# Another prologue for a two-layer attention and MLP kernel: input ahead of weights, a fixed order for the first norm, V by two token tiles, scratch matmuls, and other places for the next inputs

## The chip, the cores and the metric

The kernel runs on one core of one Trainium2 chip. The metric is device time in microseconds (us), as the median of several executions. "PE" is the matmul engine, "PEld" its weight load, "DVE" the vector engine, "ACT" the scalar engine, "POOL" the third compute engine, and "SP" the engine from which most DMAs are issued.

## The reference, cut to what matters

```python
def reference(A_x, A_wqkv, A_wo, B_x, B_W_gate, B_W_up, B_W_down):
    # A: 32 heads of 32; every token attends to 8 earlier tokens, 2 apart
    # B: relu(x @ W_gate) * (x @ W_up) @ W_down
    x = A_x                                    # 1 x 2048 x 1024, bf16
    x = x + _A_ref(_layernorm(x), A_wqkv, A_wo)
    x = x + _B_ref(_layernorm(x), B_W_gate, B_W_up, B_W_down)
    x = x + _A_ref(_layernorm(x), A_wqkv, A_wo)
    x = x + _B_ref(_layernorm(x), B_W_gate, B_W_up, B_W_down)
    return x
```

## The kernel before

The 2048 tokens are worked on in four blocks of 512 (four tiles of 128). The host code of the kernel builds a list of pairs (time, function) called `ev`, sorts it by time and calls the functions in that order; the times are the author's plan, in us. Instructions of PE and the DMAs of SP are chained in the order of these calls. Other engines' instructions are put in order by the framework's scheduler unless `tc.issue_after` fixes it.

In all the argument, a *group* is eight matmuls of 512 columns, one for each eighth of the 1024 inputs. At full rate a group takes 1.73 us.

The prologue is what comes before the first Q matmul: load block 0, normalise its four tiles (statistics of two on DVE, of two on ACT), turn them with PE transposes (eight a tile), copy the turned tiles out, and compute V of block 0 in eight groups.

```python
    def load_x(b):
        for t in range(b * TPB, (b + 1) * TPB):
            if b == 0 and t % 2:
                nc.scalar.dma_start(x_tiles[t][:], x_dram[t * P:(t + 1) * P, :])
            else:
                sp_dma(x_tiles[t][:], x_dram[t * P:(t + 1) * P, :])

    load_x(0)
    # ... (cut)
    def ln_first():
        hold = {"xnT": xnT_pool.tile([P, TPB, KC, P], BF16, tag="xnT", name="xnT_first")}
        xna = big_tile([P, TPB, D], "xn_first", True)
        for t in range(TPB):
            xt = x_tiles[t]
            xn = xna[:, t, :]
            if t % 2 == 0:
                mv, rstd = ln_dve_stats(xt)
                nc.vector.tensor_scalar(xn, xt[:], mv[:, 0:1], rstd[:], op0=ALU.subtract, op1=ALU.mult)
            else:
                # ... (cut: sums by two ACT passes, small operations on DVE, power on POOL)
                nc.scalar.activation(xn, xt[:], ACT.Identity, scale=rstd[:], bias=nb[:])
            tp = psum.tile([P, KC, P], BF16, tag="acc", name="tp")
            for c in range(KC):
                nc.tensor.transpose(tp[:, c, :], xn[:, c * P:(c + 1) * P], ident[:])
            if t % 2 == 0:
                nc.vector.tensor_copy(hold["xnT"][:, t, :, :], tp[:])
            else:
                nc.scalar.copy(hold["xnT"][:, t, :, :], tp[:])
        return hold
    # ... (cut)
    def v_steps(n, ln, key, early=False):
        # ... one of these for each of the 8 column chunks c:
                for kc in range(KC):
                    mm(acc[:], lhsT=slab[(key, g)][:, kc, col:col + P], rhs=ln["xnT"][:, :, kc, :],
                       start=(kc == 0), stop=(kc == KC - 1))
                tail_act[0] = nc.scalar.copy(st["vT"][:, c, :], acc[:]).ins
    # ... (cut: the plan of block 0)
    t_v0 = 17.0
    ev.append((0.45, lambda: load_x(1)))
    spread(v_steps(0, ln_a[0], "v0", early=True), t_v0, GRP)
    ln1(1, 18.0, t_qk0 + 2.0, True, 2.6, range(TPB))
    ev.append((t_qk0 - 4.0, lambda: load_x(2)))
    # ... products of q and k on DVE (mults), their reductions L on PE (reds)
    ev.append((t_qk1 + 0.5 * GRP, reds[KC - 2]))
    ev.append((t_qk1 + 1.5 * GRP, reds[KC - 1]))
    ev.append((t_qk1 + 1.6 * GRP, lambda: softmax(0)))
    ln1(2, 37.0, t_qk1 + 2.0, True, 4.5)
```

## Time and profile before

| | before |
|---|---|
| median of 3 executions | 1636.67 us (1636.62 to 1637.32) |
| span in the profile | 1635.0 us |
| PE busy | 1616.4 us |
| first transpose, first V matmul, first Q matmul | 8.81, 15.04, 30.95 us |
| V of block 0, from its first matmul to the first Q | 15.91 us, where 8 x 1.73 = 13.84 is due |

PE is busy 99% of the span, so time can be won only where PE idles or runs slowly. The list of PE's waits in the kernel before says where it idles (columns: what waited, for what, us in total, times, longest):

```profile
PE tp L298 <- DVE xn_first L280: 8.8, 1, 8.8
PE tp L298 <- ACT xn_first L295: 1.2, 2, 0.9
PE acc_v L120 <- ACT xnT_first L302: 1.1, 1, 1.1
PE dacc L120 <- DVE x L582: 0.8, 1, 0.8
PE L L120 <- DVE prod L395: 0.5, 1, 0.5
```

Three of the five belong to the prologue. The last is a reduction L that waits for the last product of block 0. The timeline of PE in the kernel before shows them in place (start, us from first to last, engine, line, operation, out<-in, sizes, count, and in brackets the idle time before it and what ended it):

```profile
8.81 1.03 PE L298 MATMUL tp<-ident,xn_first 128*128 128x128 bf16 x8 [8.81 <-DVE xn_first L280]
...
15.04 16.07 PE L120 MATMUL acc_v<-xnT_first,w_v 128*128 128x512 bf16 x64 [1.10 <-ACT xnT_first L302]
30.95 1.89 PE L120 MATMUL acc_q<-xnT_first,w_qk_q 128*128 128x512 bf16 x8
...
62.78 1.89 PE L120 MATMUL acc_q<-xnT_a,w_qk_q 128*128 128x512 bf16 x8
64.60 0.62 PE L120 MATMUL L<-prod,sel 128*32 128x512 bf16 x8
65.15 1.95 PE L120 MATMUL acc_q<-xnT_a,w_qk_q 128*128 128x512 bf16 x8
67.63 0.62 PE L120 MATMUL L<-prod,sel 128*32 128x512 bf16 x8 [0.54 <-DVE prod L395]
...
147.66 1.89 PE L120 MATMUL acc_g<-xnT_b,w_g 128*128 128x512 bf16 x8
```

What this line does not show is that V starts slowly. The weight loads of V in the kernel before, from the timeline of PEld, do: a weight load accompanies each matmul, so the distance between two of them is the time of a matmul.

```profile
15.42 0.15 PEld L120 LDWEIGHTS <-w_v 128*128 128x128 bf16 x1 [0.28 <-issue]
15.85 0.15 PEld L120 LDWEIGHTS <-w_v 128*128 128x128 bf16 x1 [0.28 <-issue]
```

They lie 0.427 us apart up to 19.3 us, and 0.216 us apart from then on: half rate, then full rate. The page's row of granted clock is full in this stretch all the same, so it cannot be taken as the proof that PE runs at full rate early in a kernel.

### The profile page before, as it was taken

The numbers are of one execution on the slowest core, as the hardware profiler recorded it, in microseconds if no ns is written. First come the engines' busy times: TensorE is split into PE (matmuls) and PEld (weight loads), VectorE is DVE, ScalarE is ACT, GpSimd is POOL, SyncE is SP. The second block draws the span as 40 slices with busy tenths as digits, with TensorE's granted clock in tenths as the row PEclk, the third lists the DMA queues.
The fourth block names the chain that finished last, engine by engine and source line by source line (L and its number), as shares of the span: only waits on it lengthen the run. The fifth ranks groups of instructions, "written<-read, shape, count | busy, mean of one in ns | idle before, by whom it ended". The sixth has DMA issues, their size and how long they took to land.

```text
span 1635.0 us, 18583 instructions
## 1 busy us (share of the span) xinstructions
PE 1616.4 (99%) x7527; PEld 777.6 (48%) x7576; DVE 1060.9 (65%) x923; ACT 507.7 (31%) x1047; POOL 255.7 (16%) x220
## 2 busy tenths in 40 slices
PE   7999999999999999999999999999999999999999
PEld 3554445444554445444454444544445444444444
DVE  3699999986397936949279492794828948211211
ACT  5745322433241423405134051340513311131110
POOL 2411103301160102201052010520105100000000
PEclk9999999999999999999999999999999999999999
DMA  9569557755567475764856647577474764655451
GB/s 297 93 179 240 163 170 217 197 161 175 178 187 203 155 209 167 197 177 155 232 162 185 178 151 230 179 185 215 150 226 160 205 204 154 206 156 179 155 166 66
DMA packets 371222, 296.81 MB, mean 182 GB/s; under 512 B 142400, under 2 KB 351296, under 8 KB 370240
## 3 DMA queue, kind: packets, MB, share of 16 engines
q1 hardware_dynamic: 370848, 295.10, 62.0%
q8 instruction: 59, 0.97, 0.3%
q10 hardware_dynamic: 288, 0.52, 0.1%
q14 instruction: 27, 0.22, 0.0%
HBM read 256.77 MB, written 21.00 MB: 170 GB/s over the span
## 4 chain that ended last, share of the span: by engine, by line
PE 92%; DVE 4%; ACT 2%; issue 1%; DMA 1%; POOL 0%; ACTq 0%; SPq 0%; DVEq 0%
PE acc_g L120 24%; PE acc_u L120 24%; PE dacc L120 22%; PE acc_v L120 6%; PE acc_wo L120 6%; PE acc_k L120 5%; PE acc_q L120 5%; DVE t L423 2%; DVE ac L433 1%; DMA x<-in_A_x_dram 1%; ACT xn_a L227 1%; ACT xn_a L228 1%; DVE pv L485 0%; PE L L120 0%; DVE x L530 0%
## 5 line engine op out<-in xcount | busy, mean ns | idle before, releaser
L120 PE MATMUL acc_g<-xnT_b,w_g 128*128 128x512 bf16 x1792 | 423.4, 379 | 0.0
L120 PE MATMUL acc_u<-xnT_b,w_u 128*128 128x512 bf16 x1792 | 423.3, 379 | 0.0
L120 PE MATMUL dacc<-w_d,hT 128*128 128x512 bf16 x1759 | 386.5, 379 | 2.5 <-DVE x L582 0.8
L554 ACT ACTIVATE r<-acc_g 128x512 bf16<-128x512 f32 x224 | 133.5, 596 | 746.9 <-PE acc_g L120 746.7
L555 DVE TENSOR_TENSOR hT<-acc_u,r 128x512 bf16<-128x512 f32 x224 | 153.7, 686 | 314.2 <-PE acc_u L120 313.4
L120 PEld LDWEIGHTS <-hT 128*128 128x128 bf16 x1792 | 175.3, 98 | 212.4 <-issue 1.1
L120 PEld LDWEIGHTS <-w_g 128*128 128x128 bf16 x1792 | 174.8, 98 | 212.8 <-issue 3.0
L120 PEld LDWEIGHTS <-w_u 128*128 128x128 bf16 x1792 | 175.4, 98 | 211.4
L423 DVE TENSOR_TENSOR t<-q,k 128x2048 f32<-128x2048 bf16 x84 | 191.7, 2290 | 8.6 <-ACT k L362 5.8
L433 DVE TENSOR_TENSOR ac<-ac,t 128x2048 f32<-128x2048 f32 x84 | 191.8, 2283 | 0.4
L367 POOL COPY kh<-k 128x14 bf16<-128x14 bf16 x64 | 82.1, 1288 | 480.5 <-ACT k L362 480.5
L582 DVE TENSOR_TENSOR x<-dacc,x 128x512 bf16<-128x512 f32 x64 | 42.5, 687 | 164.0 <-PE dacc L120 164.0
L485 DVE TENSOR_TENSOR pv<-a,vhm 128x4096 bf16<-128x4096 bf16 x64 | 145.2, 2282 | 0.0
L120 PE MATMUL acc_wo<-w_o,oT 128*128 128x512 bf16 x496 | 111.0, 379 | 0.8
L232 POOL TENSOR_TENSOR st_b<-st_b,neg_half 128x1 f32<-128x1 f32 x29 | 56.5, 1957 | 297.9 <-ACT st_b L231 297.9
L232 POOL TENSOR_TENSOR st_a<-st_a,neg_half 128x1 f32<-128x1 f32 x32 | 40.5, 1273 | 318.1 <-ACT st_a L231 317.9
L366 POOL COPY k<-kh 128x14 bf16<-128x14 bf16 x48 | 71.3, 1485 | 65.4 <-DVE t L423 43.8
L120 PEld LDWEIGHTS <-oT 128*128 128x128 bf16 x512 | 50.1, 98 | 60.3
L486 DVE TENSOR_TENSOR pv<-pv 128x2048 bf16<-128x2048 bf16 x64 | 77.4, 1214 | 0.2
L358 ACT CAST q<-acc_q 128x512 bf16<-128x512 f32 x64 | 37.6, 587 | 72.9 <-PE acc_q L120 72.9
L322 ACT CAST vT<-acc_v 128x512 bf16<-128x512 f32 x64 | 37.4, 585 | 70.8 <-PE acc_v L120 70.8
L227 ACT ACTIVATE xn_b<-x 128x1024 bf16<-128x1024 bf16 x29 | 30.3, 1046 | 92.1 <-DVE x L530 92.1
(125 smaller groups left out, 1204.5 us busy)
## 6 DMA issues: line engine op xcount, KB each, us to landing
w_g<-in_B_W_gate_dram SPq DMA_DIRECT2D x56, 1024.0 KB, 6.6
w_u<-in_B_W_up_dram SPq DMA_DIRECT2D x56, 1024.0 KB, 5.3
w_d<-in_B_W_down_dram SPq DMA_DIRECT2D x48, 1024.0 KB, 5.7
w_o<-in_A_wo_dram SPq DMA_DIRECT2D x16, 1024.0 KB, 7.1
vhm<-v_d SPq DMA_DIRECT2D x32, 284.0 KB, 6.8
v_d<-vT SPq DMA_DIRECT2D x8, 1024.0 KB, 9.6
oT<-o_d SPq DMA_DIRECT2D x32, 256.0 KB, 4.3
w_d<-in_B_W_down_dram SPq DMA_DIRECT2D x16, 512.0 KB, 4.2
```

Of the source, the lines that this page charges most:

```text
L120: tail_pe[0] = nc.tensor.matmul(*args, **kwargs).ins
L227: nc.scalar.activation(xn, xt[:], ACT.Square, accum_out=sq)
L232: nc.gpsimd.tensor_tensor(rstd, vpe, neg_half[:, 0:1], op=ALU.pow)
L366: nc.gpsimd.tensor_copy(k[:, 0:HALO], khalo[n - 1][:, c, :])
L367: nc.gpsimd.tensor_copy(khalo[n][:, c, :], k[:, BLK:BLK + HALO])
L423: nc.vector.tensor_tensor(t[:], i0, i1, op=ALU.mult)
L433: nc.vector.tensor_tensor(o, ac[:], t[:], op=ALU.add)
L485: nc.vector.tensor_tensor(tt[:], a_bc, v_sh, op=ALU.mult)
L486: nc.vector.tensor_tensor(tt[:, 0:4], tt[:, 0:4], tt[:, 4:8], op=ALU.add)
L554: tail_act[0] = nc.scalar.activation(r[:], acc[:], ACT.Relu).ins
L555: nc.vector.tensor_tensor(hold["hT"][:, j, :], accs["u"][:], r[:], op=ALU.mult)
L582: nc.vector.tensor_tensor(xs, ac[t], xs, op=ALU.add)
```

## The change

Its intent is to have V, and so the long unbroken stream of PE, begin sooner and at full rate. It has seven parts:

- (a) Tile 0 of the input comes in two halves, one on each of two queues; tile 2 comes on the ACT queue, tiles 1 and 3 on SP's (before: 1 and 3 on ACT's, 0 and 2 on SP's).
- (b) The norm of block 0 runs in a fixed order on each engine (`on`, `dv`); tiles 0, 1 and 3 have their statistics on DVE, tile 2 on ACT.
- (c) Fourteen scratch matmuls of ones run on PE while it has nothing to do. Nothing reads their result.
- (d) V is computed for tiles 0 and 1 first (chunks 0 to 5), then for tiles 2 and 3, then chunks 6 and 7 for all four. Tiles 2 and 3 are turned inside V.
- (e) The inputs of blocks 1 and 2 are both asked for after the fourth slab of Q and K weights: for block 2 that is sooner, for block 1 later. The norm of block 1 is interleaved with block 0's products in a fixed order.
- (f) The last L reduction and the softmax of block 0 come one group later.
- (g) Loads for the PV stage, the ACT statistics of blocks 2 and 3 and the input of block 3 move later. One small ACT instruction on the ones is new too (not shown); the ACT table load that it could bring forward starts at 1.70 us in both kernels.

```diff
@@ loading (a)
-            if b == 0 and t % 2:
+            if t == 0:
+                sp_dma(x_tiles[t][:, 0:SLAB], x_dram[t * P:(t + 1) * P, 0:SLAB])
+                nc.scalar.dma_start(x_tiles[t][:, SLAB:D], x_dram[t * P:(t + 1) * P, SLAB:D])
+            elif t == 2:
                 nc.scalar.dma_start(x_tiles[t][:], x_dram[t * P:(t + 1) * P, :])
@@ scratch (c) and order (b)
+    ones = const.tile([P, SLAB], BF16, name="ones")
+    nc.vector.memset(ones[:], 1.0)
+    def scratch(count):
+        sc = psum_l.tile([P, W, P], F32, tag="L", name="scratch")
+        for _ in range(count):
+            with pe_group():
+                mm(sc[:, 0:WH, :], lhsT=ones[:, 0:P], rhs=ones[:], start=True, stop=True)
@@ ln_first (helpers cut; "v" is DVE, "a" is ACT)
+        scratch(14)
+        bn(0, 0)
+        bn(0, 1)
+        aggr(0)
+        bn(1, 0)
+        bn(1, 1)
+        aggr(1)
+        st1 = act_stats(2)
+        apply(0)
+        turn(0)
+        apply(1)
+        copy(0, "v", 0, KC // 2)
+        copy(0, "a", KC // 2, KC)
+        turn(1)
+        act_vpe(2, st1)
+        copy(1, "v", 0, KC // 2)
+        copy(1, "a", KC // 2, KC)
+        bn(3, 0)
+        bn(3, 1)
+        apply(2)
+        aggr(3)
+        apply(3)
+        hold["later"] = {2: (lambda: (turn(2), copy(2, "a"))),
+                         4: (lambda: (turn(3), copy(3, "v", 0, KC // 2), copy(3, "a", KC // 2, KC)))}
@@ v_first (d)
+        plan = [(c, 0, 2) for c in range(6)] + [(c, 2, 4) for c in range(6)] + [(c, 0, 4) for c in range(6, KC)]
+        # for each (c, t0, t1): cols = slice(t0 * P, t1 * P)
+                        mm(acc[:, cols], lhsT=slab[("v0", c // 4)][:, kc, (c % 4) * P:(c % 4 + 1) * P],
+                           rhs=ln["xnT"][:, t0:t1, kc, :], start=(kc == 0), stop=(kc == KC - 1))
@@ the plan (e), (f), (g)
-    t_v0 = 17.0
+    t_v0 = 9.5
-    ev.append((0.45, lambda: load_x(1)))
-    ln1(1, 18.0, t_qk0 + 2.0, True, 2.6, range(TPB))
-    ev.append((t_qk0 - 4.0, lambda: load_x(2)))
+    ev.append((t_v0 + GRP * 5 + 0.5, lambda: load_x(1)))
+    ev.append((t_v0 + GRP * 5 + 0.6, lambda: load_x(2)))
+    # ... statistics, apply and turn of block 1, one tile at a time
-    ev.append((t_qk1 + 1.5 * GRP, reds[KC - 1]))
-    ev.append((t_qk1 + 1.6 * GRP, lambda: softmax(0)))
-    ln1(2, 37.0, t_qk1 + 2.0, True, 4.5)
+    ev.append((t_qk1 + 2.5 * GRP, reds[KC - 1]))
+    ev.append((t_qk1 + 2.6 * GRP, lambda: softmax(0)))
+    ln1(2, t_qk0 + 10.0, t_qk1 + 5.0, True, 4.5)
```

More of the change, by code (lines that the diff above doesn't have):

```diff
@@ L1 @@
-from contextlib import ExitStack, contextmanager
+from contextlib import ExitStack, contextmanager, nullcontext
 import concourse.bass as bass
@@ L95, with dv @@
     tail_pe = [None]
+    tail_dve = [None]
+    def dv(f, *args, **kwargs):
+        if tail_dve[0] is None:
+            tail_dve[0] = f(*args, **kwargs).ins
+        else:
+            with tc.issue_after(tail_dve[0]):
+                tail_dve[0] = f(*args, **kwargs).ins
     tail_sp = [None]
@@ L223, in f @@
                 if t in dve:
-                    hold[t] = ln_dve_stats(xt)
+                    hold[t] = ln_dve_stats(xt, which == "a")
                     return
                 sx, sq, nm2, vpe, rstd, mr = (hold["st"][:, t, i:i + 1] for i in range(6))
-                nc.scalar.activation(xn, xt[:], ACT.Square, accum_out=sq)
-                nc.scalar.activation(xn, xt[:], ACT.Identity, accum_out=sx)
+                with (tc.issue_after(tail_act[0]) if early else nullcontext()):
+                    nc.scalar.activation(xn, xt[:], ACT.Square, accum_out=sq)
+                    nc.scalar.activation(xn, xt[:], ACT.Identity, accum_out=sx)
                 nc.scalar.activation(nm2, sx, ACT.Square, scale=1.0 / D)
@@ L239, in f @@
                     mv, rstd = hold[t]
+                    if which == "a":
+                        dv(nc.vector.tensor_scalar, hold["xn"][:, t, :], x_tiles[b * TPB + t][:], mv[:, 0:1], rstd[:],
+                           op0=ALU.subtract, op1=ALU.mult)
+                        return
                     gate[0] = nc.vector.tensor_scalar(hold["xn"][:, t, :], x_tiles[b * TPB + t][:], mv[:, 0:1], rstd[:],
@@ L258, in ln_steps, with ln_dve_stats, run @@
         return [stats(t) for t in range(TPB)], [apply(t) for t in range(TPB)], turn, hold
-    def ln_dve_stats(xt):
+    def ln_dve_stats(xt, ordered):
+        def run(f, *args, **kwargs):
+            if ordered:
+                dv(f, *args, **kwargs)
+            else:
+                f(*args, **kwargs)
         bst = stat_pool.tile([P, 2, 6], F32, tag="bst", name="bst")
-        nc.vector.bn_stats(bst[:, 0, :], xt[:, 0:512])
-        nc.vector.bn_stats(bst[:, 1, :], xt[:, 512:1024])
+        run(nc.vector.bn_stats, bst[:, 0, :], xt[:, 0:512])
+        run(nc.vector.bn_stats, bst[:, 1, :], xt[:, 512:1024])
         mv = stat_pool.tile([P, 2], F32, tag="mv", name="mv", bufs=4)
-        nc.vector.bn_aggr(mv[:], bst[:].rearrange("p a b -> p (a b)"))
+        run(nc.vector.bn_aggr, mv[:], bst[:].rearrange("p a b -> p (a b)"))
         vpe = stat_pool.tile([P, 1], F32, tag="vpe1", name="vpe1")
-        nc.vector.tensor_scalar(vpe[:], mv[:, 1:2], EPS, None, op0=ALU.add)
+        run(nc.vector.tensor_scalar, vpe[:], mv[:, 1:2], EPS, None, op0=ALU.add)
         rstd = stat_pool.tile([P, 1], F32, tag="rstd1", name="rstd1", bufs=4)
@@ L274, in ln_first @@
         xna = big_tile([P, TPB, D], "xn_first", True)
-        for t in range(TPB):
-            xt = x_tiles[t]
-            xn = xna[:, t, :]
-            if t % 2 == 0:
-                mv, rstd = ln_dve_stats(xt)
-                nc.vector.tensor_scalar(xn, xt[:], mv[:, 0:1], rstd[:], op0=ALU.subtract, op1=ALU.mult)
-            else:
-                st1 = stat_pool.tile([P, 2], F32, tag="st1", name="st1")
-                nc.scalar.activation(xn, xt[:], ACT.Identity, accum_out=st1[:, 0:1])
-                nc.scalar.activation(xn, xt[:], ACT.Square, accum_out=st1[:, 1:2])
-                mean = stat_pool.tile([P, 1], F32, tag="mean1", name="mean1")
-                nc.vector.tensor_scalar(mean[:], st1[:, 0:1], 1.0 / D, None, op0=ALU.mult)
-                nvar = stat_pool.tile([P, 1], F32, tag="nvar1", name="nvar1")
-                nc.vector.scalar_tensor_tensor(nvar[:], st1[:, 0:1], mean[:], st1[:, 1:2], op0=ALU.mult, op1=ALU.subtract)
-                vpe = stat_pool.tile([P, 1], F32, tag="vpe1", name="vpe1")
-                nc.vector.tensor_scalar(vpe[:], nvar[:], -1.0 / D, EPS, op0=ALU.mult, op1=ALU.add)
-                rstd = stat_pool.tile([P, 1], F32, tag="rstd1", name="rstd1", bufs=4)
-                nc.gpsimd.tensor_tensor(rstd[:], vpe[:], neg_half[:, 0:1], op=ALU.pow)
-                nb = stat_pool.tile([P, 1], F32, tag="nb1", name="nb1")
-                nc.vector.scalar_tensor_tensor(nb[:], mean[:], -1.0, rstd[:], op0=ALU.mult, op1=ALU.mult)
-                nc.scalar.activation(xn, xt[:], ACT.Identity, scale=rstd[:], bias=nb[:])
-            tp = psum.tile([P, KC, P], BF16, tag="acc", name="tp")
-            for c in range(KC):
-                nc.tensor.transpose(tp[:, c, :], xn[:, c * P:(c + 1) * P], ident[:])
-            if t % 2 == 0:
-                nc.vector.tensor_copy(hold["xnT"][:, t, :, :], tp[:])
-            else:
-                nc.scalar.copy(hold["xnT"][:, t, :, :], tp[:])
@@ new lines, in ln_first, with on, small @@
+        last = {}
+        def on(eng, f, *args, **kwargs):
+            if eng == "v":
+                dv(f, *args, **kwargs)
+            elif eng in last:
+                with tc.issue_after(last[eng]):
+                    last[eng] = f(*args, **kwargs).ins
+            else:
+                last[eng] = f(*args, **kwargs).ins
+        def small(name, bufs=4):
+            return stat_pool.tile([P, 1], F32, tag="f" + name, name=name, bufs=bufs)
+        mean, vpe, rstd, bst = {}, {}, {}, {}
@@ new lines, in bn, with aggr @@
+        def bn(t, half):
+            if half == 0:
+                bst[t] = stat_pool.tile([P, 2, 6], F32, tag="bst", name="bst")
+            on("v", nc.vector.bn_stats, bst[t][:, half, :], x_tiles[t][:, half * SLAB:(half + 1) * SLAB])
+        def aggr(t):
+            mv = stat_pool.tile([P, 2], F32, tag="mv", name="mv", bufs=4)
+            on("v", nc.vector.bn_aggr, mv[:], bst[t][:].rearrange("p a b -> p (a b)"))
+            vpe[t], mean[t] = small("vpe1"), mv[:, 0:1]
+            on("v", nc.vector.tensor_scalar, vpe[t][:], mv[:, 1:2], EPS, None, op0=ALU.add)
+            power(t)
@@ new lines, in power, with act_stats, act_vpe @@
+        def power(t):
+            rstd[t] = small("rstd1")
+            on("g", nc.gpsimd.tensor_tensor, rstd[t][:], vpe[t][:], neg_half[:, 0:1], op=ALU.pow)
+        def act_stats(t):
+            st1 = stat_pool.tile([P, 2], F32, tag="st1", name="st1")
+            on("a", nc.scalar.activation, xna[:, t, :], x_tiles[t][:], ACT.Identity, accum_out=st1[:, 0:1])
+            on("a", nc.scalar.activation, xna[:, t, :], x_tiles[t][:], ACT.Square, accum_out=st1[:, 1:2])
+            return st1
+        def act_vpe(t, st1):
+            mn = small("mean1")
+            on("v", nc.vector.tensor_scalar, mn[:], st1[:, 0:1], 1.0 / D, None, op0=ALU.mult)
+            nvar = small("nvar1")
+            on("v", nc.vector.scalar_tensor_tensor, nvar[:], st1[:, 0:1], mn[:], st1[:, 1:2], op0=ALU.mult, op1=ALU.subtract)
+            vpe[t], mean[t] = small("vpe1"), mn[:]
+            on("v", nc.vector.tensor_scalar, vpe[t][:], nvar[:], -1.0 / D, EPS, op0=ALU.mult, op1=ALU.add)
+            power(t)
@@ new lines, in apply, with turn, copy @@
+        def apply(t):
+            on("v", nc.vector.tensor_scalar, xna[:, t, :], x_tiles[t][:], mean[t], rstd[t][:],
+               op0=ALU.subtract, op1=ALU.mult)
+        tps = {}
+        def turn(t):
+            tps[t] = psum.tile([P, KC, P], BF16, tag="acc", name="tp")
+            for c in range(KC):
+                with pe_group():
+                    tail_pe[0] = nc.tensor.transpose(tps[t][:, c, :], xna[:, t, c * P:(c + 1) * P], ident[:]).ins
+        def copy(t, eng, c0=0, c1=KC):
+            f = nc.vector.tensor_copy if eng == "v" else nc.scalar.copy
+            on(eng, f, hold["xnT"][:, t, c0:c1, :], tps[t][:, c0:c1, :])
@@ new lines, in ln_first @@
+        warm = small("warm")
+        on("a", nc.scalar.activation, warm[:], ones[:, 0:1], ACT.Identity)
+        scratch(14)
[16 more added lines that the diff above has]
+        bn(3, 0)
@@ L325, in v_steps, with v_first, f_, f @@
         return [f_(c) for c in range(KC)]
+    def v_first(ln):
+        st = att[0]
+        plan = [(c, 0, 2) for c in range(6)] + [(c, 2, 4) for c in range(6)] + [(c, 0, 4) for c in range(6, KC)]
+        def f_(i, c, t0, t1):
+            def f():
+                if i == 0:
+                    st["vT"] = big_tile([P, KC, BLK], "vT_0", True)
+                acc = psum.tile([P, BLK], F32, tag="acc", name="acc_v")
+                cols = slice(t0 * P, t1 * P)
+                with pe_group():
+                    for kc in range(KC):
+                        mm(acc[:, cols], lhsT=slab[("v0", c // 4)][:, kc, (c % 4) * P:(c % 4 + 1) * P],
+                           rhs=ln["xnT"][:, t0:t1, kc, :], start=(kc == 0), stop=(kc == KC - 1))
+                tail_act[0] = nc.scalar.copy(st["vT"][:, c, cols], acc[:, cols]).ins
+                if i in ln["later"]:
+                    ln["later"][i]()
+            return f
+        at, out = 0.0, []
+        for i, (c, t0, t1) in enumerate(plan):
+            out.append((at, f_(i, c, t0, t1)))
+            at += GRP * (t1 - t0) / TPB
+        return out
     def store_v(n):
@@ L394, in f @@
                 i0, i1 = qk_bcast(n, c, 0, W)
-                nc.vector.tensor_tensor(prods[c][:], i0, i1, op=ALU.mult)
+                dv(nc.vector.tensor_tensor, prods[c][:], i0, i1, op=ALU.mult)
             return f
@@ L598 @@
     GRP = 1.73
-    GRP = 1.73
     def spread(steps, at, gap):
@@ L642 @@
     t_gu0 = t_v3 + GRP * KC
-    want_v("v0", t_v0 + GRP * KC / 2, t_qk0)
+    want_v("v0", t_v0 + GRP * 5, t_qk0)
     want_qk("qk01", t_v1)
     want_v("v123", t_v3 + GRP * KC / 2, t_gu0)
-    ev.append((0.45, lambda: load_x(1)))
-    ev.append((0.5, zero_v))
-    spread(v_steps(0, ln_a[0], "v0", early=True), t_v0, GRP)
-    ln1(1, 18.0, t_qk0 + 2.0, True, 2.6, range(TPB))
-    ev.append((t_qk0 - 4.0, lambda: load_x(2)))
+    for at, f in v_first(ln_a[0]):
+        ev.append((t_v0 + at, f))
+    ev.append((t_v0 + GRP * 5 + 0.5, lambda: load_x(1)))
+    ev.append((t_v0 + GRP * 5 + 0.6, lambda: load_x(2)))
+    ev.append((t_v0 + GRP * 5 + 0.7, zero_v))
+    stats, apply, turn, ln_a[1] = ln_steps(1, "a", True, range(TPB))
+    for t in range(TPB):
+        ev.append((t_qk0 + (1.0, 2.0, 2.2 * GAP0, 4.2 * GAP0)[t], stats[t]))
+        ev.append((t_qk0 + (1.9 + 2 * t) * GAP0 - 0.1, apply[t]))
+        ev.append((t_qk0 + (1.9 + 2 * t) * GAP0, turn(t)))
     ev.append((t_qk0 + 1.5, store_v(0)))
-    ev.append((t_qk0 + 2.1, lambda: load_x(3)))
+    ev.append((t_qk0 + 18.0, lambda: load_x(3)))
     spread(qk_steps(0, ln_a[0], "qk01"), t_qk0, GAP0)
@@ L659 @@
             ev.append((t_qk0 + GAP0 * (2 * c + 4.5), reds[c]))
-    spread(load_v_steps(0), t_qk0 + 5.0, 6.0)
+    spread(load_v_steps(0), t_qk0 + 19.0, 1.0)
     ev.append((t_qk1 + 0.5 * GRP, reds[KC - 2]))
-    ev.append((t_qk1 + 1.5 * GRP, reds[KC - 1]))
-    ev.append((t_qk1 + 1.6 * GRP, lambda: softmax(0)))
-    ln1(2, 37.0, t_qk1 + 2.0, True, 4.5)
+    ev.append((t_qk1 + 2.5 * GRP, reds[KC - 1]))
+    ev.append((t_qk1 + 2.6 * GRP, lambda: softmax(0)))
+    ln1(2, t_qk0 + 10.0, t_qk1 + 5.0, True, 4.5)
     spread(qk_steps(1, ln_a[1], "qk01"), t_qk1, GRP)
```

## The prediction

> **What bounds the kernel now.** The page's first part has PE busy 1616 of 1635 us. The list of waits charges PE with five: 8.8 us for the first normalised tile, 1.2 for the next, 1.1 for the transposed input, 0.54 at one L reduction (67 us), 0.8 at a down projection (314 us). The timeline has the first V matmul at 15.04 us and the first Q matmul at 30.95; from there PE hardly stops, 1.73 us per eight 512-column matmuls. So the change can win only what lies before 31 us, plus small waits.
>
> V takes 15.9 us where 8 x 1.73 = 13.8 is due: until about 19 us its weight loads lie 0.427 us apart, later 0.216. The matmuls run at half rate though the granted clock reads 1.0, as the Trainium skill says ("TensorE: Matmul & The Clock Gate", "The HAM clock gate": cold until about 3.4 us of sustained activity). That costs 2.1 us.
>
> **What changes, costed.**
> 1. Before, four tiles are normalised and turned before any V: x lands at 4.5-5.7, first transpose 8.81, last copy ends 15.0. Now V needs tiles 0 and 1 only. From about 4.0: two statistics (0.62 each) and two small operations, to 5.7; tile 1's during tile 0's 0.55-0.8 us power, to 7.3; apply 0.55, to 8.0; transposes 0.6-0.9; small operations and half copies; V at 10.2 (estimate). W_v's first slab should land near 8.5: by then 2.1 MB had moved before.
> 2. Fourteen scratch matmuls (14 x 0.427 = 6 us) on an idle PE: V starts warm, the 2.1 us goes.
> 3. V pays: 16 transposes now sit inside it (1-1.7 us), 48 more matmuls cost little each. V: 13.8 + 1.7 = 15.5, ending near 25.7 against 30.95: 5.2 us won. Tiles 2 and 3 should be applied near 13.4, needed near 15.
> 4. Block 1's input now queues behind a slab that waits for W_v: it lands around 26-28. Its statistics and applies (8 us of DVE) move among block 0's eight products (2.3 us each, one per 4.1 us of PE): 26 of 33 us. Room enough. ACT was full from 36 to 60 us with statistics of blocks 2 and 3; block 3's now come later, so K copies and products are punctual.
> 5. The last L reduction comes one group later: the 0.54 us wait goes, but softmax starts 1.1 us later relative to PE. DVE is full from 75 to 200 us, so its chain gains 4 us while PE gains 5.7. The attention output's first tile landed near 117.4, PE takes it at 120.0: 2.6 us of slack, 1.6 used. DVE idles 6 us before 207 and catches up.
>
> **Sum.** 5.2 + 0.54 = about 5.8 us: 1636.7 - 5.8 = **1630.9 us**. Eight in ten: 1629.2 to 1633.0. Chances: faster by over 2% 0.005, within 2% 0.99, slower 0.005.
>
> **What would show it.** First V matmul at 9.4-11 us (1); 256-column matmuls about 0.11 us apart from the start (2); first Q near 25.7 (3); no PE wait on products or block 1's input, block 1's Q starting near 57 instead of 62.8 (4, 5); no PE wait before the output projection near 114; from 250 us everything shifted by the same 5-6 us, the 0.8 us wait kept.
>
> **What would make it wrong.** x or W_v landing later; PE cold again between scratch and transposes (up to 2 us); 256-column matmuls bound by weight loads (+1 us or more); block 1's late input pushing products and softmax until the output projection waits; the MLP input's DMA transposes, with under 2 us of slack at 147.7, coming late.

## The result, and the profile after

Four executions of each kernel were taken in the same rounds. Ratios in this document are the mean time of one kernel's fast runs over that of the other's of the same rounds, so not quite the ratio of the medians.

| | before | after |
|---|---|---|
| median (lowest to highest) | 1636.97 us (1636.62 to 1637.32) | 1630.12 us (1630.08 to 1630.63) |
| ratio | | 0.9959 (95%: 0.9944 to 0.9973) |
| span in the profile | 1635.0 | 1628.4 |
| first transpose | 8.81 | 7.45 |
| first V matmul | 15.04 | 9.69 |
| first Q matmul | 30.95 | 24.69 |
| first Q of block 1 | 62.78 | 56.52 |
| first gate matmul of block 0 | 147.66 | 140.79 |

The kernel is 0.4% faster: 6.85 us between the medians, where 5.8 were predicted. That is within the 2% that count as the same here, but the interval of the ratio leaves out 1. The list of PE's waits in the changed kernel:

```profile
PE scratch L129 <- DVE ones L296: 1.5, 1, 1.5
PE dacc L129 <- DVE x L700: 0.8, 1, 0.8
PE acc_v L129 <- DVE xnT_first L103: 0.6, 1, 0.6
PE tp L364 <- DVE xn_first L103: 0.4, 1, 0.4
```

What was 8.8 + 1.2 + 1.1 is now 1.5 + 0.6 + 0.4. The first of these is a wait before scratch work, so it costs nothing by itself, and the scratch matmuls have turned idle time into busy time of no use: busy PE has to be read by tile here. The L wait is gone, and the 0.8 of the down projection stays. The timeline of PE in the changed kernel (columns as above):

```profile
1.52 5.91 PE L129 MATMUL scratch<-ones 128*128 128x512 bf16 x14 [1.52 <-DVE ones L296]
7.45 0.62 PE L364 MATMUL tp<-ident,xn_first 128*128 128x128 bf16 x8
8.44 0.62 PE L364 MATMUL tp<-ident,xn_first 128*128 128x128 bf16 x8 [0.37 <-DVE xn_first L103]
9.69 2.96 PE L129 MATMUL acc_v<-xnT_first,w_v 128*128 128x256 bf16 x24 [0.63 <-DVE xnT_first L103]
12.48 0.61 PE L364 MATMUL tp<-ident,xn_first 128*128 128x128 bf16 x8
12.93 1.91 PE L129 MATMUL acc_v<-xnT_first,w_v 128*128 128x256 bf16 x16
14.68 0.61 PE L364 MATMUL tp<-ident,xn_first 128*128 128x128 bf16 x8
15.12 9.73 PE L129 MATMUL acc_v<-xnT_first,w_v 128*128 128x256 bf16 x72
24.69 1.89 PE L129 MATMUL acc_q<-xnT_first,w_qk_q 128*128 128x512 bf16 x8
...
56.52 1.89 PE L129 MATMUL acc_q<-xnT_a,w_qk_q 128*128 128x512 bf16 x8
58.34 0.62 PE L129 MATMUL L<-prod,sel 128*32 128x512 bf16 x8
58.88 3.67 PE L129 MATMUL acc_q<-xnT_a,w_qk_q 128*128 128x512 bf16 x16
62.49 0.62 PE L129 MATMUL L<-prod,sel 128*32 128x512 bf16 x8
...
140.79 1.89 PE L129 MATMUL acc_g<-xnT_b,w_g 128*128 128x512 bf16 x8
```

Three things are to be seen. V starts 15.04 - 9.69 = 5.35 us sooner. From V's first matmul to the first Q it takes 24.69 - 9.69 = 15.0 us instead of 15.91; eight transposes now take 0.62 us instead of 1.03, so PE is at full rate when they come. And the second L reduction (62.49) has no bracket, hence no wait. From here the sum closes: 5.35 + 0.91 + 0.54 = 6.80, and the gate matmuls come 147.66 - 140.79 = 6.87 us sooner. Nothing of it is given back later: the 0.8 us wait of the down projection moved from 315.03 to 308.13 us, by 6.90.

One input of this is the first statistics on DVE. First the line of the kernel before, from the timeline of DVE:

```profile
4.71 0.69 DVE L262 BATCH_NORM_STATS2 bst<-x 128x6 f32<-128x512 bf16 x1 [4.71 <-DMA x<-in_A_x_dram]
```

and that of the changed kernel, from the same view:

```profile
3.60 0.69 DVE L100 BATCH_NORM_STATS2 bst<-x 128x6 f32<-128x512 bf16 x1 [2.13 <-DMA x<-in_A_x_dram]
```

The half tile gets there 1.1 us sooner than the whole one did.

### The profile page after: what moved, and what is told of

It is laid out like the page before. It is cut to its first block, busy times and chain, and to the rows that moved or that the text cites. A ratio compares the mean times of both kernels' runs of the same rounds, so it can differ in the third digit from the quotient of the medians.

```text
span 1628.4 us, 18703 instructions
## 1 busy us (share of the span) xinstructions
PE 1618.6 (99%) x7589; PEld 782.2 (48%) x7638; DVE 1062.6 (65%) x926; ACT 506.1 (31%) x1050; POOL 255.7 (16%) x220
## 4 chain that ended last, share of the span: by engine, by line
PE 95%; DVE 4%; issue 1%; DMA 0%; POOL 0%; DVEq 0%
PE acc_g L129 24%; PE acc_u L129 24%; PE dacc L129 22%; PE acc_v L129 7%; PE acc_k L129 6%; PE acc_q L129 6%; PE acc_wo L129 6%; DVE t L541 2%; DVE ac L551 1%; PE L L129 1%; DVE pv L603 0%; DVE x L648 0%; DVE pv L604 0%; DVE ac L541 0%; DMA x<-in_A_x_dram 0%
## 5 line engine op out<-in xcount | busy, mean ns | idle before, releaser
L480 ACT CAST k<-acc_k 128x512 bf16<-128x512 f32 x64 | 37.3, 583 | 63.0 <-PE acc_k L129 62.8
```

## The experiments

The profile says what moved. It does not say which of the parts moved it, because several of them act on the same few microseconds. Twelve kernels were run. The table has all of them. "Against before" is the median less the median of the kernel before on the same chip; those medians lay between 1636.70 and 1637.24 us, so differences below half a microsecond between rows of different chips are not read. The starts of V and Q are from the profiled execution, one for each kernel. The interval of the ratio includes 1, no change, for e2, e3 and e9.

| run | median us | against before | first V | first Q |
|---|---|---|---|---|
| changed kernel | 1630.12 | -6.85 | 9.69 | 24.69 |
| e1_no_scratch | 1631.76 | -5.48 | 10.10 | 26.37 |
| e2_before_scratch | 1638.38 | +1.14 | 15.77 | 31.98 |
| e3_no_split | 1635.81 | -1.43 | 14.46 | 30.22 |
| e4_red_early | 1630.14 | -7.10 | 9.66 | 24.67 |
| e5_x0_whole | 1632.44 | -4.57 | 10.67 | 27.00 |
| e6_free_order | 1632.48 | -4.53 | 11.06 | 26.74 |
| e7_x1_early | 1630.84 | -6.17 | 9.89 | 24.89 |
| e8_scratch_20 | 1630.58 | -6.43 | 9.61 | 24.62 |
| v1_single_tile | 1632.21 | -4.49 | 9.71 | 26.52 |
| e9_before_fill | 1635.72 | -1.17 | 15.30 | 29.11 |
| e10_no_split_fill | 1633.56 | -3.33 | 14.36 | 28.17 |
| v2_hold_back | 1631.46 | -5.43 | 9.71 | 26.16 |

All gave correct results. At first the theory was that of the prediction: the parts act one by one and add up (an earlier V, plus about 2 us for a PE that is at full rate when V starts). The rivals were that one part does nearly all, or that parts hang together.

### e1: the changed kernel without scratch matmuls

```diff
-        scratch(14)
```

> The changed kernel without its 14 scratch matmuls. Theory A (the scratch matmuls warm PE's clock): the 32 transposes and the first V groups run at half rate for about 4 us of PE activity, as in the kernel before: the first V matmul moves from 9.69 to about 10.2 us, weight loads of V's first groups lie about 0.213 us apart instead of 0.11, Q starts near 27.2 instead of 24.69; time 1632.2 to 1633.0 (2.1 to 2.8 us more than the changed kernel). Rival B (the transposes warm PE anyway, or the half rate of before had another cause): V at 9.7 to 10.2 with 0.11 us spacing from the start, time within 0.7 us of 1630.1.

Measured: 1631.76 us (1631.39 to 1632.37), less than expected. The first V matmuls in this kernel, from the timeline of PE, are to be compared with 2.96 us for the same 24 in the changed kernel:

```profile
10.10 4.22 PE L129 MATMUL acc_v<-xnT_first,w_v 128*128 128x256 bf16 x24 [0.52 <-DVE xnT_first L103]
```

The scratch matmuls are worth 1.68 us of Q's start: 4.22 - 2.96 = 1.26 for V's first matmuls, and 0.41 for V's start (the first transpose is 0.11 later, and from there to V takes 0.30 longer). The prediction had read 2.1 us for a cold V from the kernel before; here a cold V costs 1.26, so that price is not a constant.

### e2: the kernel before with scratch matmuls and nothing else

```diff
     def ln_first():
         # ...
+        scratch(17)
         for t in range(TPB):
```

> The kernel before with 17 scratch matmuls ahead of its first transposes and nothing else of the change. Theory A: first V matmul still near 15 us (14.6 to 15.0, as transposes run at full rate), but V takes 13.8 instead of 15.9 us: Q starts near 28.6 instead of 30.95; time 1634.3 to 1635.0. Rival B: V still 15.9 us, time 1636.5 to 1637.3. If the wait at the last L reduction grows because ACT stays where it was, up to 0.5 us of the gain is lost there (then 1635.0 to 1635.5).

Measured: 1638.38 us (1637.51 to 1638.77), ratio 1.0006 (0.9991 to 1.0021). The expectation fell: not faster at all. The windows of this kernel show what happened (columns: stretch, its length, busy us and count of PE, PEld, DVE, ACT, POOL, then granted clock, DMA share and GB/s). The stretches are 3.41 us long and laid so that one ends where the clock fell, at 13.83 us by the clock record of the trace (it keeps the moments at which the granted clock changed):

```profile
7.00:10.41 3.41, 1.67 (x13) 0.74 (x11) 2.06 (x12) 2.85 (x6) 1.96 (x4) 1.00 1.10 355
10.41:13.83 3.42, 1.19 (x18) 1.02 (x19) 1.85 (x5) 1.91 (x3) 0.55 (x1) 1.00 1.07 375
13.83:17.24 3.41, 2.31 (x12) 1.24 (x11) 0.00 (x0) 1.73 (x2) 0.00 (x0) 0.50 1.05 387
17.24:20.65 3.41, 3.41 (x9) 1.22 (x8) 0.00 (x0) 0.59 (x1) 0.00 (x0) 0.50 1.05 388
```

The granted clock is 0.50 from 13.83 to 20.65 us. PE was brought to full rate by the scratch matmuls, then had little to do (transposes that wait for the norm), and fell back to half rate 1.9 us before V began at 15.77. So V took 31.98 - 15.77 = 16.2 us, as slow as before, and it also began 0.73 us later (why was not traced). From this came a third theory: *scratch matmuls are worth something only if PE is kept busy from them to the real stream; the early start of V is what keeps it busy.* It is tested by e9 and e10.

### e3: the changed kernel with V whole

```diff
-        hold["later"] = {2: (lambda: (turn(2), copy(2, "a"))),
-                         4: (lambda: (turn(3), copy(3, "v", 0, KC // 2), copy(3, "a", KC // 2, KC)))}
+        turn(2)
+        copy(2, "a")
+        turn(3)
+        # ... copies of tile 3
+        hold["later"] = {}
-        plan = [(c, 0, 2) for c in range(6)] + [(c, 2, 4) for c in range(6)] + [(c, 0, 4) for c in range(6, KC)]
+        plan = [(c, 0, 4) for c in range(KC)]
```

> The changed kernel with V in eight groups of 512 columns after all four tiles, all else kept. Theory A: V begins when tile 3 is copied, near 13.9 us instead of 9.69, and takes 13.8 us instead of 15.16: Q near 27.7 instead of 24.69, time 1632.8 to 1633.4 (about 3 us more). Rival (the split is not worth its transposes and half matmuls, the fixed order and the loads are what counts): time within 1 us of 1630.1.

Measured: 1635.81 us (1635.6 to 1636.0). Without the split only 1.4 us of the gain are left, far less than expected. The clock fell here too, for 6.8 us from 11.6 on, so V took 15.76 us.

### e9: the kernel before, with scratch matmuls also between the transposes

```diff
+        scratch(17)
         for t in range(TPB):
             # ... after the transposes of tile t
+            scratch((5, 0, 7, 5)[t])
```

> The run of the kernel before with scratch matmuls came out slower, not faster: its granted clock fell to 0.50 from about 13.9 to 20.4 us, after the transposes had left PE idle for most of 8 to 14 us. Theory C: once warmed, PE is set back to half rate when it idles too much over some us, so scratch matmuls ahead of the norm only pay if PE then stays busy. Here 5, 7 and 5 scratch matmuls more fill the gaps after the transposes, nothing else changes. C: granted clock 1.0 throughout, V's weight loads 0.216 us apart from its first group, V takes 13.8 us instead of 16.2; V starts at 15.8 to 16.2 us and Q at 29.6 to 30.1; time 1635.4 to 1636.4, 2 to 3 us under the run without the fill. Rival D (the clock falls at about 14 us whatever PE does, say by the all-ones data or a fixed time after warming): clock 0.50 again and time 1638 to 1639.

Measured: 1635.72 us (1635.36 to 1635.95), 1.2 us under the kernel before (ratio 0.9991, 0.9978 to 1.0005) and, each against the kernel before on its chip, 2.3 us under e2. All four executions have a mean clock of 1.000, where e2's four have 0.996 to 0.999. The windows of this kernel (columns as above):

```profile
8.31:11.72 3.41, 2.68 (x30) 1.84 (x31) 1.99 (x7) 1.82 (x3) 1.75 (x4) 1.00 1.10 354
11.72:15.13 3.41, 3.23 (x22) 1.47 (x20) 0.76 (x2) 2.93 (x3) 0.19 (x1) 1.00 1.05 386
```

The clock stays up, and V takes 29.11 - 15.30 = 13.8 us, the 8 x 1.73 that are due. The third theory holds: what e2 lacked was work for PE between the scratch matmuls and V. Q starts 1.84 us sooner than before, of which 1.2 us arrive at the end; PE waits 0.9 us for L reductions instead of 0.54, and the rest was not traced.

### e10: e3 with scratch matmuls filling the same gaps

```diff
         turn(1)
+        scratch(9)
         # ...
         turn(2)
+        scratch(3)
         # ...
         turn(3)
+        scratch(4)
```

> The changed kernel with V whole after four tiles came out 5.7 us slower, where I expected 3: its clock too fell to 0.50, from about 11.8 to 18.2 us. Here 9, 3 and 4 scratch matmuls fill PE's gaps between the transposes. Theory C: clock 1.0 throughout, V starts near 14.0 to 14.5 us (the first two pairs of transposes and copies at full rate), takes 13.8 us, Q near 28.0 to 28.4; time 1633.2 to 1633.8, 2 to 2.5 us under the run without the fill; the split of V itself is then worth 3.1 to 3.7 us and the clock that it keeps up the rest. Rival D: clock 0.50 again, time about 1635.8.

Measured: 1633.56 us (1633.32 to 1633.88). The same stretch in both kernels, first in e3:

```profile
8.19:11.60 3.41, 0.92 (x14) 0.75 (x15) 3.17 (x11) 1.17 (x2) 0.55 (x1) 1.00 1.10 364
```

and in e10:

```profile
8.19:11.60 3.41, 2.71 (x21) 1.33 (x20) 3.24 (x10) 1.17 (x2) 0.55 (x1) 1.00 1.09 365
```

With 0.92 us busy the clock fell at 11.6; with 2.71 it stayed at 1.00. e10 gives the split its own price. With the clock up in both, the first Q is at 28.17 us without the split and at 24.69 with it: 3.5 us for starting V on two tiles instead of four. The remaining 2.05 us of e3's loss (30.22 - 28.17) are the clock's.

### e5: the changed kernel, tile 0 in one piece

```diff
-            if t == 0:
-                sp_dma(x_tiles[t][:, 0:SLAB], x_dram[t * P:(t + 1) * P, 0:SLAB])
-                nc.scalar.dma_start(x_tiles[t][:, SLAB:D], x_dram[t * P:(t + 1) * P, SLAB:D])
-            elif t == 2:
+            if b == 0 and t % 2:
```

> The changed kernel with block 0's input loaded as before: tile 0 whole on one queue, tiles 1 and 3 on the other, tile 2 on the first. Theory: tile 0 in two halves at the heads of both queues is what brought the first statistics from 4.71 to 3.60 us, and the chain of tile 1 carries this to V. So here the first statistics start at 4.5 to 4.8 us and the first V matmul at 10.5 to 10.8, time 1630.9 to 1631.3. Rival (tile 1's own landing or W_v's landing near 8.7 us sets V's start): V within 0.3 us of 9.69, time within 0.3 us of 1630.1.

Measured: three executions at 1632.40 to 1632.71 us with a mean granted clock of 0.999, and one at 1631.08 with 1.000. The one is what was expected, the three are not. The first statistics start at 4.57 us and V at 10.67, both about 0.98 later, as expected. The edit also puts tiles 1 to 3 back on their old queues, so this is the price of part (a) as a whole; that the halves make it is argued from the start of the statistics. In the profiled execution, one of the three, the clock is at half from 10.4 to 13.8 us and costs another 1.3 us (Q starts 2.31 late in all). The same kernel can thus fall or not fall from one execution to the next.

### e6: the changed kernel with the order of the norm left to the scheduler

```diff
     def dv(f, *args, **kwargs):
-        if tail_dve[0] is None:
+        if True:
             tail_dve[0] = f(*args, **kwargs).ins
             # ...
-            elif eng in last:
+            elif False:
                 with tc.issue_after(last[eng]):
```

> The changed kernel without the fixed order on DVE, ACT and POOL in block 0's norm (and without it for block 1's norm and the products). The scheduler then puts tile 3's statistics and tile 2's small operations ahead of the applies of tiles 0 and 1. Theory: V waits 1.0 to 1.6 us longer (first V matmul 10.7 to 11.3 us), time 1631.0 to 1631.8. Rival (the order does not matter, the tiles come in the order of their landing anyway): V within 0.3 us of 9.69, time within 0.3 us of 1630.1.

Measured: 1632.48 us (1632.16 to 1632.78). V starts at 11.06 us, 1.37 later, as expected: the order is worth that by itself. Beyond it, all four executions have a mean clock of 0.999. The windows of this kernel:

```profile
5.98:9.39 3.41, 1.32 (x11) 0.57 (x10) 3.38 (x14) 1.20 (x3) 2.31 (x5) 1.00 1.04 358
9.39:12.80 3.41, 2.90 (x22) 2.23 (x20) 1.70 (x5) 1.17 (x2) 0.08 (x2) 0.51 1.08 371
```

The clock is at half for the whole of the second stretch. The longest idle time of PE before it is 2.09 us (from the end of the scratch matmuls to the first transpose), so a much shorter gap than 3.4 us was enough here.

### e8: twenty scratch matmuls instead of fourteen

```diff
-        scratch(14)
+        scratch(20)
```

> The changed kernel with 20 scratch matmuls instead of 14, to see when the clock turns. In the changed kernel all weight loads of the scratch matmuls lay 0.427 us apart up to 6.62 us, and the transposes at 7.44 us ran at full rate. If the clock turns between 6.6 and 7.4 us, the spacing falls to 0.216 us there and the scratch ends near 8.4 to 8.7 us; then tile 0's transposes wait about 1 us and V starts 0.3 to 0.8 us later: time 1630.3 to 1631.0. If it turns only later, or with the pause, all 20 are slow: they end near 10.1 us, V starts near 11.5, time about 1632.

Measured: 1630.58 us (1630.18 to 1630.9), the same as fourteen within what can be read. V starts at 9.61, not later as expected: the weight loads of the scratch matmuls lie 0.216 us apart from 5.2 us on, sooner than the expectation looked for, while in the changed kernel, with the same code up to there, they lay 0.427 apart up to 6.62. So it is not the count of matmuls that brings full rate. Fourteen are enough where V follows soon.

### e4: the last reduction at its old place

```diff
-    ev.append((t_qk1 + 2.5 * GRP, reds[KC - 1]))
-    ev.append((t_qk1 + 2.6 * GRP, lambda: softmax(0)))
+    ev.append((t_qk1 + 1.5 * GRP, reds[KC - 1]))
+    ev.append((t_qk1 + 1.6 * GRP, lambda: softmax(0)))
```

> The changed kernel with the last L reduction of block 0 back after the second Q group, as before. My prediction said that its move took away the 0.54 us wait. If so the wait comes back here (0.3 to 0.9 us on PE before the last L reduction, time 1630.5 to 1631.0). Rival, which the trace after suggests: the products come sooner against PE because ACT no longer makes block 3's statistics there; the last product ended at 59.70 us, and PE would come to this reduction near 60.6 us, so no wait comes back and the time stays within 0.3 us of 1630.1, while softmax of block 0 starts near 61.4 instead of 63.2 us.

Measured: 1630.14 us (1629.96 to 1630.77). The timeline of PE in this kernel has the reduction back behind one group of Q:

```profile
58.86 1.95 PE L129 MATMUL acc_q<-xnT_a,w_qk_q 128*128 128x512 bf16 x8
60.73 0.62 PE L129 MATMUL L<-prod,sel 128*32 128x512 bf16 x8
```

There is no bracket at 60.73, so no wait. The prediction had put the end of the 0.54 us wait down to the later reduction; that was wrong. The wait ends because the last product ends sooner relative to PE: at 67.58, 4.80 us after block 1's first Q, before, and at 59.70, 3.18 us after it, in the changed kernel. What the profile shows of the reason is that ACT, which converts the k that the product reads, was busy 21.0 of 21.0 us between 36 and 57 us before and 17.8 in the changed kernel. Step 4 of the prediction had named this ("block 3's now come later, so K copies and products are punctual"), but did not credit it with the 0.54 us. That ACT is the cause was argued from these numbers, not tried alone. The later reduction gives nothing here, and its cost (the softmax starts at 63.16 instead of 61.41) does not reach PE either.

### e7: the inputs of blocks 1 and 2 at their old places

```diff
-    ev.append((t_v0 + GRP * 5 + 0.5, lambda: load_x(1)))
-    ev.append((t_v0 + GRP * 5 + 0.6, lambda: load_x(2)))
+    ev.append((0.45, lambda: load_x(1)))
+    ev.append((t_qk0 - 4.0, lambda: load_x(2)))
```

> The changed kernel with the inputs of blocks 1 and 2 issued where they were before (block 1 ahead of the fourth Q/K slab, block 2 near the end of V). Theory: their place is off the critical path: in the changed kernel DVE waits for block 1's input until 25.8 us, but the first product is not needed before 29.5 us; so block 1's statistics start near 20 us here, no PE wait appears and the time stays within 0.3 us of 1630.1. Rival (the later load of block 1 buys PE time by letting the fourth Q/K slab through sooner): PE waits at the first K group near 26.4 to 28 us, time up by 0.5 us or more.

Measured: 1630.33, 1630.55, 1631.13 us at a clock of 1.000, and 1632.60 at 0.999. In the profiled execution (1630.55) the weights of Q and K now come late behind the input of block 1, as a line of PEld's timeline shows:

```profile
27.66 0.64 PEld L129 LDWEIGHTS <-w_qk_k 128*128 128x128 bf16 x4 [0.46 <-DMA w_qk_k<-in_A_wqkv_dram]
```

So the rival's wait at the first K group came, though small: from the first group of Q to the second it takes 3.69 us instead of 3.45. The new places are worth at most half a microsecond, near the limit of what can be read. Whether they have a part in the one fall of four was not shown.

### v1 and v2: can V start on a single tile?

Both start V on tile 0 alone (chunks 0 to 3), then tile 1, then the rest. In v1 the loads are otherwise as they were, with the second half of the block loaded behind W_v's first slab. In v2 tiles 2 and 3 were also held back until 5.8 us and W_v's second slab until 6.6, to see whether W_v's first slab is slow because it shares the DMA engines.

```diff
-        plan = [(c, 0, 2) for c in range(6)] + [(c, 2, 4) for c in range(6)] + [(c, 0, 4) for c in range(6, KC)]
+        plan = [(c, 0, 1) for c in range(4)] + [(c, 1, 2) for c in range(4)] + [(c, 0, 2) for c in range(4, KC)] + \
+               [(c, 2, 4) for c in range(KC)]
+    ev.append((0.05, lambda: load_x(0, (2, 3))))
@@ v2 only: tiles 2 and 3 are loaded over a value that DVE writes once it is done with tile 0
+        dv(nc.vector.memset, x_tiles[2][:, 0:1], 0.0)
```

> A further step of my own on the changed kernel: V begins with tile 0 alone (four groups of 128 columns), then tile 1 alone, then four groups of tiles 0 and 1, then all eight groups of tiles 2 and 3; tiles 0 and 1 are loaded in halves on both queues, W_v's first slab ahead of tiles 2 and 3; ACT makes tile 1's statistics, DVE those of tiles 0, 2 and 3; 12 scratch matmuls. Theory (V's start and no more is what the front costs): first V matmul near 8.0 us, if W_v's first slab lands by then (estimate 7, from 8.7 with 0.5 MB less ahead of it); V takes 13.8 plus 24 transposes of 0.056 us plus small costs, so Q starts at 23.3 to 23.9 instead of 24.69, time 1628.9 to 1629.6. Rival (V's start is then set by W_v's landing, or 128-column matmuls are bound by their weight loads, or tile 2 and 3 come late): V at 8.7 or later, or waits inside V, time 1629.8 or more.

> My single-tile version failed because W_v's first slab, issued at 1.74 us, landed only at 9.64: the loads issued after it (tiles 2 and 3, W_v's second slab) took their share of the DMA engines at once, 7.9 to 8.2 us to landing each. And its clock fell to 0.50 in most runs. Here a one-column write by VectorE into tile 2, after tile 0's statistics at about 5.4 us, holds back tiles 2 and 3 and all loads behind them, and three scratch matmuls fill PE's gap behind tile 0's transposes (14 ahead of them). If the sharing is the cause, W_v's first slab (1.5 MB with the two tiles, at 0.35 to 0.4 MB per us) lands at 6.3 to 7.3 us, the first V matmul comes at 7.8 to 8.6, Q at 23.2 to 24.0, the clock stays at 1.0, time 1628.5 to 1629.5. If not: V at 9 us or later, time 1630 or more.

Measured: v1 1629.89 and 1631.01 us at a clock of 1.000, and 1632.21 to 1632.30 in three executions at 0.999; v2 1631.46 us (1631.2 to 1631.86), all at 1.000. Neither is shown to beat the changed kernel. The timeline of PE, in v1:

```profile
9.71 1.89 PE L129 MATMUL acc_v<-xnT_first,w_v 128*128 128x128 bf16 x16 [2.24 <-DMA w_v<-in_A_wqkv_dram]
```

and in v2:

```profile
9.71 1.07 PE L129 MATMUL acc_v<-xnT_first,w_v 128*128 128x128 bf16 x16 [1.31 <-DMA w_v<-in_A_wqkv_dram]
...
14.77 1.92 PE L129 MATMUL acc_v<-xnT_first,w_v 128*128 128x256 bf16 x16 [0.69 <-DMA w_v<-in_A_wqkv_dram]
```

In both, V now waits for its weights. W_v's first slab of 1 MB, asked for at 1.7 us, landed at about 9.66 in both. But v2 tests the sharing less than was meant: by the packets in the traces, nothing of tiles 2 and 3 moved before 6.56 us in v1 either (6.75 in v2). The DMA engines were not full before that: from 4.0 to 6.5 us their busy share was 0.76 (v1) and 0.78 (v2), against 1.04 in the changed kernel. And the slab lands in sixteen parts, each with an event of its own in the trace: in v2 twelve parts were there by 8.07 us and four came only at 9.47 to 9.66, while in the changed kernel, which asks at 2.21 us with the second slab right behind, all sixteen came from 8.38 to 8.76. So sharing with later loads does not explain the wait up to 6.5 us, and why some parts come so late stays open. The changed kernel has its weights at 8.76 and starts V at 9.69, so by the weights V could start at most 0.9 us sooner there.

## Why the prediction was right, and where it was not

The predicted total was 5.8 us and the measured one 6.85; 1630.12 lies inside the predicted range. Point by point:

**"So the change can win only what lies before 31 us, plus small waits": right.** Q starts 6.26 us sooner, the L wait of 0.54 is gone, and everything later is shifted by 6.9.

**Step 1, start of V: right mechanism, 0.5 us too late.** Predicted 10.2, measured 9.69. The first statistics begin at 3.60, not at about 4.0. W_v's slab was expected near 8.5 us and landed at 8.76, so it was not what V waited for.

**Step 2, half rate ends: right in the sum, wrong as it was costed.** V's 2.1 us of half rate did go. But the prediction counted them as the scratch matmuls' own ("V starts warm, the 2.1 us goes"), as if fourteen matmuls on an idle PE did it. Seventeen such matmuls alone, in the kernel before, gain nothing (e2: +1.14 us); taken from the changed kernel they cost 1.4 (difference of the gains) to 1.7 us (Q's start). They are worth something because the fixed order, the halves and the split give PE work before the clock falls. The prediction named this under what would make it wrong ("PE cold again between scratch and transposes"), and did not see that it was the hinge of the change.

**Step 3, what V pays: too high.** 1 to 1.7 us were allowed for 16 transposes inside V; they take 2 x 0.45 = 0.9 us (12.48 to 12.93 and 14.68 to 15.12). V took 15.0 instead of 15.5. Steps 1 and 3 together are the missing microsecond: 0.5 + 0.5.

**Step 4, block 1: right.** Its statistics start at 25.77 us in the changed kernel (the expectation was that the input would land at 26 to 28) and block 1's Q starts at 56.52 without a wait (expected near 57).

**Step 5, "the 0.54 us wait goes": right effect, wrong cause.** e4 puts the reduction back and the wait stays away. That is the step of the prediction that failed; the last product comes 1.62 us sooner relative to block 1's first Q (3.18 instead of 4.80 us), which is nearer to its step 4. The expected harm, a softmax 1.1 us later relative to PE, was there (1.12) but had slack.

**Where the gain comes from, then.** The parts do not add up, because two of them act through the clock as well:

| part | direct, by the start of V or Q | and through the clock |
|---|---|---|
| V on two tiles (e10 against changed, e3 against e10) | 3.5 us | 2.05 us |
| fixed order of the norm (e6) | 1.4 us | 0.7 us |
| loading of block 0's input (e5) | 1.0 us | 1.3 us, in three executions of four |
| scratch matmuls (e1; e2) | 1.7 us in the changed kernel, nothing alone | |
| places of the next inputs (e7) | at most 0.5 us | 1 execution of 4 fell |
| later reduction (e4) | nothing | |

**How the clock falls.** The five profiles that show a fall agree with what the Trainium skill says ("TensorE: Matmul & The Clock Gate", "What's actually happening"): the activity window is 3413 ns long and free-running. The clock records of the traces give the moments of full, half and again full rate: 7.00, 13.83 and 20.65 us in e2; 4.79, 11.61 and 18.44 in e3; 6.96, 10.37 and 13.79 in e5; 6.02, 9.44 and 12.85 in e6; 5.80, 9.22 and 12.63 in v1. Every step is 3.41 or 6.83 us, one window or two. The scratch matmuls start at 1.52 us in all the runs that have them, and yet the first full rate comes anywhere from 4.79 (e3) to 7.05 us (the changed kernel), so the start of the window is not tied to the kernel's. That fits the executions of e5, e7 and v1 that fall or do not fall with the same code.

How little activity is too little was read from these windows afterwards, and was not tried by a run of its own. Laid from these moments, the five windows before a fall hold 0.93, 1.19, 1.20, 1.32 and 1.67 us of busy PE (e3, e2, v1, e6, e5). The poorest windows that did not end in a fall hold 1.67 (the first of e2's above), 2.00 (e9), 2.04 (e7) and 2.11 (e4). So windows with 2 us or more, about 60%, held in every profile that was read, those with 1.32 or less fell, and at 1.67 there is one of each kind. The one that fell, in e5:

```profile
6.96:10.37 3.41, 1.67 (x18) 0.95 (x17) 2.74 (x10) 1.66 (x3) 0.90 (x4) 1.00 1.10 349
```

The tie is one of the view, which counts each run of matmuls up to a modelled end: 0.62 us for eight transposes that start 56 ns apart. An estimate without these ends takes the starts from the traces and gives each matmul the distance at which such matmuls follow each other (56, 109 and 216 ns for 128, 256 and 512 columns at full rate). Then the five windows that fell hold 0.75 to 1.16 us, and the poorest that held 1.34 (e2), 1.60 (e4) and 1.69 (e7): one limit between a third and two fifths of the window would fit every profile here, with transposes counted. The Trainium skill says of transposes ("TensorE: Matmul & The Clock Gate", "Part 4: PE-mode transpose") that they do not count as busy "the same way". Left out of this estimate, they give no clean limit: e6 fell with 0.74 us of other matmuls and e4 held with 0.70. That is too close to decide whether they count. The same window of the changed kernel, which is the poorest of its prologue after the scratch matmuls,

```profile
7.05:10.46 3.41, 2.38 (x24) 1.48 (x23) 2.81 (x9) 1.24 (x3) 1.35 (x3) 1.00 1.10 354
```

holds 2.38 us. It is above the doubtful stretch, but not by far: with V a microsecond later, as in e5 and e6, it is not.

What stays open: whether the clock falls by that count of activity, why some parts of W_v's first slab come so late in v1 and v2, and whether freeing ACT alone would have ended the L wait. Part (g) was not taken out by itself.

## What to carry to other kernels

Matmuls on nothing, to bring PE to full rate before its work, pay only if PE then stays busy until that work begins; look at the granted clock and at PE's busy time in stretches of 3.4 us from the warm-up to the stream (here 2 us of busy PE in each were enough and 1.3 were not). Starting the first long stage on the part of the input that is ready first (here two of four tiles) won the most, both by itself and by keeping PE at full rate. When parts of a change act on the same microseconds, take each out of the whole and also put it alone into the old kernel: only the two together showed here that the scratch matmuls gain something only where PE is kept busy from them to V.

## What the Trainium skill lacked or had wrong

- "TensorE: Matmul & The Clock Gate", "HAM oscillation — how this bites in real kernels", gives the rule "no PE-idle gaps >~3.4µs." It is too weak: in e6 the longest gap before the fall was 2.09 us, and that window held 1.32 us of busy PE (39%). The page has no figure for how much activity a window needs; here windows with up to 1.32 us of busy PE ended in half rate and those with 2.0 us or more did not, with one of each kind at 1.67.
- The same page, "Part 4: PE-mode transpose", says that full rate does not engage for transposes. Here they ran at full rate once PE had it: eight with their weight loads in 0.45 us, 56 ns each, against 107 ns each in the kernel before, at half rate (8 in 1.03 us from first to last). What may fit the page: before its full rate, in the window from 9.08 to 12.49 us (counted back from 19.32), the kernel before had 2.50 us of busy PE, all transposes, and full rate did not follow.
- The same page, "Back-to-back issue gap", has 131 ns for a stream of weight loads and matmuls of 512 columns, and calls the 216 ns an isolated gap. In the long stream here it is 216 ns: 1.73 us for eight, and the same page's "Wait — 56ns, not 53.3ns?" has that figure.
- No page that was read says that the profile's granted clock reads 1.00 before the first warm-up, while matmuls run at half rate: in the kernel before, 0.427 us each from 15.0 to 19.3 us at a clock of 1.00. It showed 0.50 only after a fall; the clock record in the trace begins with the first full rate, here at 19.32 us.
- No page that was read explains why a 1 MB slab of weights asked for at 1.7 us landed only 7.9 us later in v1 and v2, with four of its sixteen parts 1.4 us behind the others in v2, when it took 6.5 us in the changed kernel behind more bytes of input.
